# Pooled attention and two-layer network: GpSimd operations begun one per step behind the weights' conversion, bounds' matmuls behind the product with V

## The chip, the cores and the metric

The kernel runs on one core of a Trainium2 chip. The metric is the device time of one execution in microseconds (us), the median of several runs. The program has one launch; its inputs and its output lie in HBM.

## What is computed

Inputs are q, k and v (4 batches, 8 heads, 1152 positions, 64 values per head), a vector `g_ln` (512) and two weight matrices of 512x2048 and 2048x512, all float32. The reference, cut to what matters:

```
q_pool = q.reshape(B, H, S // 2, 2, D).mean(axis=3)
scores = scale * q_pool @ k^T ; attn = softmax(scores)
x   = (attn @ v), heads side by side          # 4 x 576 x 512
xn  = (x - mean) / sqrt(var + 1e-6) * g_ln
out = x + relu(xn @ w_ch1) @ w_ch2
```

## The kernel before, in words

**Tiles and steps.** Two heads of a batch make a pair `p`; there are 16 pairs, four per batch, and each is worked on in 9 steps (`C`) of 128 rows of scores, 144 steps in all. `step(i)` writes out the instructions of step `i` for every engine. There is no scheduler: each engine runs its instructions in the order in which the Python code issues them, and semaphores hold an instruction until what it reads is there. Numbers are split into two float16 halves (high and low), so that TensorE can work in float16 with float32 accuracy.

**The first batch (steps 0 to 35, `on_pe(i)` true).** In a step VectorE takes the maximum of the 1152 scores from PSUM (`emit_max`, L381), ScalarE takes the exponential (L395), TensorE transposes the result (`emit_t`, L428), ScalarE copies it back (L434), and TensorE multiplies it with V in float32 (L452). In the same steps the network's weights are loaded and converted. They come as 32 pieces of 128x1024 (`w_load`), one per step; ScalarE writes an absolute value of one half of the words (`w_bias`, L705) and three VectorE operations per piece (`w_conv`, run by `drip` at L109: a shift, then two combinations of two tiles in SBUF) bring each piece into one part of `wsl`. I call these three the conversion. In `step`, all of them are issued before the low halves of the next pair (L283, L306), which are VectorE's last work in a step.

**The weights' split.** The weights have four parts (0 and 2 of the first matrix, 1 and 3 of the second), each of four slices. When a part's maximum is known, `w_splits(part)` plans three GpSimd operations per slice, on 128x1024 float32: `w_split_a` scales (L257 `wsl<-wsl,gs` or `wsl<-wsl,wscl`), `w_split_b` writes the high half in float16 (L257 `wsl<-wsl`), `w_split_c` subtracts (L788). I call them first product, second product and difference. Parts 0 and 1 are planned in the steps that follow their scale, up to three operations in a step; parts 2 and 3 from steps 36 and 46. `w_done` counts finished slices, and a unit of the network's matmuls is issued only when its slices are counted.

**Other GpSimd work.** For every second pair it adds neighbouring rows of q (`pool_q`, L172) and copies the result (`dup_q`, L178), converts V (`take_v`, L268 to L278), and from step 32 normalises rows (`ln_r`, L551 to L557). From step 36 it computes every third low half of the probabilities (L257 `pe<-pe`, L416), the others run on VectorE (L418).

**Order by tables.** `at(i, fn)` puts a function at the end of step `i`, `pre(i, fn)` at its start.

**Bounds.** To scale a pair, ScalarE sums absolute values of k, q and v (`bound`, L191), TensorE transposes the three sums (`all_max` `one`, L207), VectorE takes their maximum (L210, L211), and TensorE spreads it over the partitions (`two`, L218). `reds` holds these two TensorE pieces for each pair, one per step. From step 36 on, `step` issues TensorE's work in this order: scores of step i+1 (L362, L370), one piece of `reds`, a product with V (`a_piece`, L464, 27 matmuls), a unit of the network (L600 or L632, `some_units`), a transpose for the next pair (`a_prep`).

Of the kernel before, what the change touches and what calls it, by code (L numbers as in the profile page):

```python
# [9 lines left out]
FP32 = mybir.dt.float32  # L10
# [14 lines left out]
def tile_pooled_attention_moe(  # L25
# [18 lines left out]
    nc = tc.nc  # L44
# [4 lines left out]
    C = S // 128  # L49
    HP = H // 2  # L50
# [18 lines left out]
    sm_p = ctx.enter_context(tc.tile_pool(name="sm", bufs=2))  # L69
# [185 lines left out]

    def scaled(dst, src, s=1.0):
        nc.gpsimd.tensor_scalar(dst, src, s, 1.0, op0=ALU.mult, op1=ALU.mult)  # L257

    def take_v(p, h):

# [75 lines left out]
    def on_pe(i):  # L336

        return 0 <= i < HP * C
# [236 lines left out]
    evacs = []  # L575
# [218 lines left out]
    def at(i, fn, *a):  # L794
        todo.setdefault(i, []).append((fn, a))
# [3 lines left out]
    def pre(i, fn, *a):  # L799
        early.setdefault(i, []).append((fn, a))  # L800
# [5 lines left out]
    for p in range(1, NP):  # L806
        i0 = (p - 1) * C
        at(max(i0 - 1, 0), load, p, "k", nc.sync)
        at(i0, load, p, "v", nc.sync)
        at(i0 + 1, bound, p, "k")  # L810
        if p % 2 == 0:
            at(i0 - 2, load_q, p, (nc.sync,))
            pre(i0 + 1, pool_q, p, nc.gpsimd)
            at(i0 + 1, dup_q, p, nc.gpsimd)
            at(i0 + 2, bound, p, "q")
        elif p == 1:
            upper = (64, 64)
            pre(0, behind_scales)
            pre(i0 + 1, pool_q, 1, nc.gpsimd, (upper,))
            at(i0 + 1, dup_q, 1, nc.gpsimd, (upper,))  # L820
            at(i0 + 2, bound, 1, "q", *upper)
        else:
            at(i0 + 1, same_q, p)
        if not on_pe(p * C):
            at(i0 + 2, bound, p, "v")
        pre(i0 + 3, scales_reduce, p, 0, 2 if on_pe(p * C) else 3)
        for n in range(2):
            at(i0 + (5, 7)[n], take_v, p, n)
        for n, (fn, u) in enumerate(PREPS):
            late = 1 if on_pe(i0) else 0  # L830
            pre(i0 + 4 + n + late, lambda fn=fn, p=p, u=u: preps.append((fn, p, u)))
# [8 lines left out]

    this = [0]

    def w_splits(part):
        for n in range(4):
            i0 = this[0] + 1 + 3 * n // 2 if part < 2 else 16 + 10 * part + 5 * n // 2
            for x, fn in ((0, w_split_a), (1, w_split_b), (2, w_split_c)):
                at(i0 + x, fn, 4 * part + n)

# [29 lines left out]
    def norm(i):  # L878

        if not norms or norms[0][1] % 2 == 0 and norms[0][0] != "h" and not room["xn"]:  # L880
            return
        b, t = norms.popleft()
        st = {}
        if b == "h":
            x = xh[t][:, 0]
            dst = xh[t][:, 1].bitcast(FP16).rearrange("p (a n) -> p a n", a=2 * KD)
        else:
            x = xb[b][:, t]
            keep = batch.setdefault(b, {})
            if t % 2 == 0:  # L890
                keep["xn", t] = x_p.tile([128, 2 * KD, 256], FP16, tag="xn", name="xn")
                room["xn"] -= 1
            dst = keep["xn", t - t % 2][:, :, 128 * (t % 2):128 * (t % 2) + 128]
        ln_a(st, x)
        ln_r(st, nc.gpsimd if i < NSTEP else nc.vector)

        def transpose():
            evacs.extend(ln_t(st, dst))

        d = 2 if i < NSTEP else 1  # L900
        at(i + d, transpose)
        if b == "h":
            at(i + d + 1, units_of_half, t)
        elif t % 2:
            at(i + d + 1, units_of, b, t)
            if t == 3 and b == 1:
                at(i + d + 1, lambda: norms.append(("h", 0)))
# [26 lines left out]
    def some_units(i):  # L934
        for _ in range(1 if i < NSTEP + 5 else 2):
            if units and w_done[units[0][0]] >= units[0][1]:
                evacs.extend(units.popleft()[2]())

    def a_piece(i):
        pieces.extend(ready.pop(i, ()))  # L940
        for u in range(2 if len(pieces) > 2 and not on_pe(i) else 1):
            if pieces:
                n = pieces.popleft()
                pt = pts[n]
                ps = emit_pv(n, bank() if u or on_pe(n) else None)
                if on_pe(n):
                    ot = pt.rearrange("p a n -> p (a n)").bitcast(FP32)[0:65, 0:128]
                    evacs.append(lambda ot=ot, ps=ps: nc.scalar.activation(
                        out=ot, in_=ps[0:65, 0:128], func=ACTF.Identity, bias=eps
                    ))  # L950
                    turned.append((n, ot))
                    continue
                evacs.extend(evac_pv(n, ps))
                evacs.append(lambda n=n: evacuated(n))

    def step(i):
        live = i < NSTEP
        this[0] = i
        for fn, a in early.pop(i, ()):
            fn(*a)  # L960
        if live:
            emit_max(i)
        if on_pe(i - 1):
            emit_t_copy(i - 1)
            steps.pop(i - 1)
        while found:
            found.popleft()()
        first = on_pe(i - 2) or on_pe(i)
        if first and not on_pe(i):
            a_piece(i)  # L970
        if on_pe(i):
            if i < 3:
                warm(16, bank())
            a_piece(i)
            a_prep()
            emit_exp(i)
        while scaled_out:
            scaled_out.popleft()()
        if i + 1 < NSTEP:
            emit_s(i + 1)  # L980
            pv_slot[0] = i + 1
        else:
            free_banks[:] = [6, 7, 0, 1, 3, 4]
            pv_slot[0] += 1
        while sums and i % 2 == sums[0][0] // 2:
            sums.popleft()[1]()
        if on_pe(i):
            while fill:
                drip()
            flush()  # L990
        else:
            flush()
            if live:
                emit_exp(i)
                emit_hi(i)
        if 0 <= i - 1 < NSTEP and not on_pe(i - 1):
            emit_lo(i - 1)
            steps.pop(i - 1)
            drip()
        norm(i)  # L1000
        while soon or len(fill) > 3:
            drip()
        if on_pe(i):
            emit_t(i)
            if reds:
                found.append(reds.popleft()())
        elif reds:
            evacs.append(reds.popleft()())
        while turned:
            n, ot = turned.popleft()  # L1010
            emit_turn(n, ot, i)
        if not on_pe(i):
            if not first:
                a_piece(i)
            some_units(i)
            a_prep()
        for fn, a in todo.pop(i, ()):
            fn(*a)

    def warm(n, ps=None):  # L1020
        ps = psum[:, 2, 0:128] if ps is None else ps[:, 0:128]
# [87 lines left out]
```

## Time and profile before

| what | us |
|---|---|
| median of 3 runs (lowest, highest) | 882.64 (880.32, 884.50) |
| profiled execution | 883.46 |
| its span, first to last instruction | 881.7 |
| PE busy | 823.7 |
| VectorE (DVE) busy | 614.7 |
| ScalarE (ACT) busy | 570.7 |
| GpSimd (POOL) busy | 349.0 |

Busy times are sums over the whole span, and the stages have different limits: the first batch with the weights' conversion, batches 1 to 3, and a tail of the network's matmuls. What a change is worth has to be read from its own stage. PE is TensorE's matmuls, PEld its weight loads; a matmul's end is modelled. Time that an engine waits is put down to the instruction that released it.

### The profile page before, as it was taken

The page shows a single profiled execution, that of the slowest core. Times are in us where ns is not written, and L with a number is a line of the kernel's source. Part 1 is how long each engine was busy: PE and PEld are TensorE (multiplying, and loading weights), DVE is VectorE, ACT ScalarE, POOL GpSimd, SP SyncE. Part 2 cuts the span into 40 slices and gives each one's busy share as a digit, 9 for nine tenths or more (in the row PEclk, how much of TensorE's full clock was granted, in tenths as well). Part 3 has the DMA queues.
Part 4 walks back from the last instruction along what each step waited for, and adds up shares of the span by engine and source line. Part 5 has one row for each costly group of instructions (what it writes and reads, how often), then busy time and mean ns, then how long its engine had stood idle before and what let it go on. Part 6 is the DMA issues. An engine that isn't in the chain of part 4 may idle for free.

```text
span 881.7 us, 21840 instructions
## 1 busy us (share of the span) xinstructions
PE 823.7 (93%) x9270; PEld 587.6 (67%) x9270; DVE 614.7 (70%) x1092; ACT 570.7 (65%) x851; POOL 349.0 (40%) x318
## 2 busy tenths in 40 slices
PE   8999899898898999898899999999999999999997
PEld 6778687686656575556666666566757576666764
DVE  4687989897777787778778777777877777532121
ACT  3988788887566686668676767676768676411110
POOL 3010634436776934364464345526343423300000
PEclk9999989899999999999999999999999999999999
DMA  6463436303589698969697969796988967600001
GB/s 187 149 207 120 129 120 183 120 1 87 105 146 181 129 173 162 201 132 181 118 222 124 196 126 215 125 179 113 196 155 158 175 113 135 121 13 13 16 10 24
DMA packets 276017, 115.97 MB, mean 132 GB/s; under 512 B 259280, under 2 KB 259280, under 8 KB 275920
## 3 DMA queue, kind: packets, MB, share of 16 engines
q1 hardware_dynamic: 275568, 113.70, 62.3%
q8 instruction: 72, 1.18, 0.5%
q10 hardware_dynamic: 352, 0.88, 0.4%
q14 instruction: 25, 0.20, 0.1%
HBM read 46.14 MB, written 4.72 MB: 58 GB/s over the span
## 4 chain that ended last, share of the span: by engine, by line
PE 51%; DVE 26%; ACT 13%; DMA 4%; issue 3%; POOL 1%; SPq 1%; ACTq 0%; POOLq 0%; DVEq 0%
PE psum L632 15%; PE psum L600 14%; DVE mx L381 7%; PE psum L464 6%; DVE hl L418 5%; PE psum L362 4%; PE psum L452 4%; ACT pe L395 3%; DVE stage L109 3%; DVE ht L614 2%; PE psum L428 2%; ACT ht L613 2%; DVE wsl L109 2%; PE psum L370 2%; DVE kt L283 1%
## 5 line engine op out<-in xcount | busy, mean ns | idle before, releaser
L381 DVE TENSOR_REDUCE mx<-psum 128x1 f32<-128x1152 f32 x144 | 194.4, 1350 | 20.6 <-ACT xb L519 7.0
L632 PE MATMUL psum<-wsl,ht 128*128 128x512 f16 x864 | 196.6, 379 | 3.9 <-DVE ht L614 3.4
L395 ACT ACTIVATE pe<-psum,nb,sc 128x1152 f32<-128x1152 f32 x144 | 188.9, 1312 | 12.0 <-DVE nb L386 10.5
L600 PEld LDWEIGHTS <-wsl 128*128 128x128 f16 x1920 | 171.9, 99 | 29.5 <-issue 9.2
L600 PE MATMUL psum<-xn,wsl 128*128 128x256 f16 x1536 | 181.7, 277 | 8.4 <-DVE xb L645 4.3
L632 PEld LDWEIGHTS <-ht 128*128 128x128 f16 x864 | 80.8, 98 | 92.3 <-issue 4.5
L409 ACT ACTIVATE hl<-pe 128x1152 f16<-128x1152 f32 x108 | 125.6, 1163 | 8.0 <-DMA pt<-hl 4.7
L362 PE MATMUL psum<-kt,qt 64*128 64x512 f16 (+1 forms) x960 | 127.4, 381 | 1.7 <-ACT pe L395 0.9
L614 DVE SCALAR_TENSOR_TENSOR ht<-psum,ht 128x512 f16<-128x512 f32 x72 | 49.8, 691 | 104.7 <-ACT ht L613 104.7
L464 PE MATMUL psum<-vt,pt 128*128 128x65 f16 (+1 forms) x3240 | 117.6, 194 | 0.0
L464 PEld LDWEIGHTS <-pt 128*128 128x128 f16 (+1 forms) x3240 | 109.5, 100 | 2.5 <-DMA pt<-hl 0.4
L418 DVE SCALAR_TENSOR_TENSOR hl<-pe,hl 128x1152 f16<-128x1152 f32 x72 | 109.3, 1518 | 0.0
L519 ACT ACTIVATE xb<-psum,r 128x64 f32<-128x64 f32 x128 | 39.7, 310 | 96.1 <-DVE r L515 89.0
L613 ACT ACTIVATE ht<-psum 128x512 f16<-128x512 f32 x72 | 42.7, 593 | 88.2 <-PE psum L600 87.9
L257 POOL TENSOR_SCALAR pe<-pe 128x1152 f32<-128x1152 f32 x36 | 42.0, 1168 | 140.1 <-ACT hl L409 135.4
L416 POOL TENSOR_TENSOR hl<-pe,hl 128x1152 f16<-128x1152 f32 x36 | 85.5, 2374 | 3.0
L452 PE MATMUL psum<-pt,vt 128*65 128x128 f32 (+1 forms) x720 | 82.1, 272 | 1.4 <-DVE qt L283 1.4
L452 PEld LDWEIGHTS psum<-pt,vt 128*65 128x65 f32 x720 | 76.1, 144 | 1.8 <-DVE qt L283 1.8
L362 PEld LDWEIGHTS <-qt 64*128 64x128 f16 (+1 forms) x960 | 39.8, 97 | 39.7 <-issue 22.3
L370 PEld LDWEIGHTS <-qt 128*128 128x128 f16 (+1 forms) x320 | 17.8, 99 | 72.5 <-issue 72.0
L370 PE MATMUL psum<-kt,qt 128*128 128x128 f16 (+1 forms) x320 | 41.4, 226 | 12.1 <-ACT xb L519 10.6
L283 DVE SCALAR_TENSOR_TENSOR qt<-psum,s,qt 128x384 f16<-128x384 f32 x48 | 29.5, 614 | 33.3 <-ACT qt L286 33.2
(116 smaller groups left out, 1003.8 us busy)
## 6 DMA issues: line engine op xcount, KB each, us to landing
stage<-in_moe_w_ch_dram SPq DMA_DIRECT2D x32, 512.0 KB, 5.1
kr<-in_k_dram SPq DMA_DIRECT2D x16, 576.0 KB, 4.5
qr<-in_q_dram SPq DMA_DIRECT2D x31, 288.0 KB, 6.2
vr<-in_v_dram SPq DMA_DIRECT2D x15, 576.0 KB, 4.7
out_dram<-xb SPq DMA_DIRECT2D x32, 128.0 KB, 2.5
pt<-hl SPq DMA_TRANSPOSE x108, 4.9
kr<-in_k_dram SPq DMA_DIRECT2D x16, 64.0 KB, 4.2
vr<-in_v_dram ACTq DMA_DIRECT2D x1, 576.0 KB, 6.7
```

What stands on the lines that cost most here:

```text
L362: nc.tensor.matmul(out=sp[o:o + w, c0:c0 + 512], lhsT=qt[r:r + 64, qa, q0:q0 + w], rhs=kt[r:r + 64, ka, h], start=(a == 0), stop=(a == 2),)
L370: nc.tensor.matmul(out=sp[o:o + w, 1024:1152], lhsT=qt[:, qa, q0:q0 + w], rhs=pair[p]["k8"][:, h], start=(qa == 0), stop=(qa == 1),)
L381: nc.vector.tensor_reduce(mx, st["s"], axis=AX.X, op=ALU.max)
L395: nc.scalar.activation(out=st["pe"], in_=st["s"], func=ACTF.Exp, scale=pair[i // C]["sc"][:, 0:1], bias=st["nb"],)
L409: nc.scalar.activation(out=hl[:, 0], in_=st["pe"], func=ACTF.Copy, scale=2.0 ** 15)
L416: nc.gpsimd.tensor_tensor(hl[:, 1], st["pe"], hl[:, 0], op=ALU.subtract)
L418: nc.vector.scalar_tensor_tensor(hl[:, 1], st["pe"], 2.0 ** 15, hl[:, 0], op0=ALU.mult, op1=ALU.subtract)
L452: nc.tensor.matmul(out=ps[0:65, q0:q0 + w], lhsT=vt[:, h, c], rhs=pt[:, 128 * u + q0:128 * u + q0 + w], start=(u == 0), stop=(u == C - 1),)
L464: nc.tensor.matmul(out=dst[:, 0:n], lhsT=lhsT, rhs=rhs, start=(u == 0 and lhsT is hi and n == 65), stop=(u == C - 1 and lhsT is lo), skip_ ...
L600: nc.tensor.matmul(out=ps[:, o:o + n], lhsT=wsl[:, 8 * w + cc, wa, f * 128:f * 128 + 128], rhs=xn[:, xa * KD + cc, 0:n], start=(m == 0), s ...
L614: lambda: nc.vector.scalar_tensor_tensor(lo, pv, 0.0, hi, op0=ALU.max, op1=ALU.subtract),
L632: nc.tensor.matmul(out=ps, lhsT=hv[0][:, ha, f, t * 128:t * 128 + 128], rhs=wsl[:, 8 * w + 4 + f // 2, wa, (f % 2) * DM:(f % 2) * DM + DM] ...
```

## The change

`gate()` is new: VectorE writes one column of a small tile, GpSimd copies it to the next column. Since both engines work in order, what GpSimd has behind the copy can't begin before VectorE has reached its write. A queue `calm` is new as well: at the end of a step one entry is taken from it, with a gate ahead of it (from step 35 on, two entries and no gate). The twelve split operations of parts 0 and 1 go through `calm`, and so do `pool_q` and `dup_q` of pairs 2 and 4; V's conversions of pairs 1 to 3 get a gate of their own. The loads of q for pairs 2 and 4 are issued two steps earlier, the splits of parts 2 and 3 planned from steps 40 and 49. From step 36 on, the piece of `reds` is issued behind the product with V.

```diff
+    def gate():
+        x = sm_p.tile([128, 2], FP32, tag="gate", name="gate", bufs=4)
+        nc.vector.memset(x[:, 0:1], 1.0)
+        nc.gpsimd.tensor_copy(x[:, 1:2], x[:, 0:1])
...
         if p % 2 == 0:
-            at(i0 - 2, load_q, p, (nc.sync,))
-            pre(i0 + 1, pool_q, p, nc.gpsimd)
-            at(i0 + 1, dup_q, p, nc.gpsimd)
+            if on_pe(i0):
+                at(i0 - 4, load_q, p, (nc.sync,))
+                at(i0 - 1, lambda p=p: calm.appendleft((lambda n: pool_q(p, nc.gpsimd), 0)))
+                at(i0, lambda p=p: calm.appendleft((lambda n: dup_q(p, nc.gpsimd), 0)))
+            else:
+                at(i0 - 2, load_q, p, (nc.sync,))
+                pre(i0 + 1, pool_q, p, nc.gpsimd)
+                at(i0 + 1, dup_q, p, nc.gpsimd)
...
         for n in range(2):
+            if on_pe(p * C):
+                at(i0 + (5, 7)[n], gate)
             at(i0 + (5, 7)[n], take_v, p, n)
...
     def w_splits(part):
         for n in range(4):
-            i0 = this[0] + 1 + 3 * n // 2 if part < 2 else 16 + 10 * part + 5 * n // 2
+            if part < 2:
+                calm.extend((fn, 4 * part + n) for fn in (w_split_a, w_split_b, w_split_c))
+                continue
+            i0 = 22 + 9 * part + 5 * n // 2
...
         elif reds:
-            evacs.append(reds.popleft()())
+            red = reds.popleft()
+            put = [None]
+            evacs.append(lambda: put[0]())
...
             if not first:
                 a_piece(i)
+            if red:
+                put[0] = red()
             some_units(i)
             a_prep()
         for fn, a in todo.pop(i, ()):
             fn(*a)
+        if calm and i < HP * C - 1:
+            gate()
+        for _ in range(1 if i < HP * C - 1 else 2):
+            if calm:
+                fn, n = calm.popleft()
+                fn(n)
```

Three places show how the instructions move. First GpSimd's queue around the add for pair 4, in steps 25 to 29; before:

```order
L257 TENSOR_SCALAR wsl<-wsl,wscl 128x1024
L257 TENSOR_SCALAR wsl<-wsl 128x1024
L257 TENSOR_SCALAR wsl<-wsl,wscl 128x1024
L172 TENSOR_TENSOR qr<-qr 128x18x64
L178 COPY qr<-qr 128x18x64
L788 TENSOR_TENSOR wsl<-wsl 128x1024
```

The same place of GpSimd's queue with the change (lines of the changed kernel, where L263 is the gate's copy, L279 V's conversion and L794 the difference):

```order
L263 COPY gate<-gate 128x1
L279 COPY vt<-vr 128x9x64
L263 COPY gate<-gate 128x1
L257 TENSOR_SCALAR wsl<-wsl,gs_84 128x1024
L263 COPY gate<-gate 128x1
L172 TENSOR_TENSOR qr<-qr 128x18x64
L263 COPY gate<-gate 128x1
L178 COPY qr<-qr 128x18x64
L263 COPY gate<-gate 128x1
L257 TENSOR_SCALAR wsl<-wsl 128x1024
```

Each large operation now has a gate's copy in front, and it is still part 0 (`gs`) that is worked on here, where it was part 1 (`wscl`).

Second, VectorE's queue in one step of the first batch with the change (L262 is the gate's write, L387 the maximum, L518 the reciprocal of the row sums; it reads as before but for L262):

```order
L262 MEMSET gate 128x1
L387 TENSOR_REDUCE mx<-psum 128x1
L518 RECIPROCAL r<-psum 128x1
L109 TENSOR_SCALAR stage<-stage 128x512
L109 SCALAR_TENSOR_TENSOR stage<-wsl,stage 128x512
L109 SCALAR_TENSOR_TENSOR wsl<-stage 128x512
L289 SCALAR_TENSOR_TENSOR qt<-psum,s,qt 128x384
```

The write stands behind a step's last work and right ahead of the next step's maximum.

Third, TensorE's queue in a later step in which a pair's bounds are transposed; before:

```order
L370 MATMUL psum<-kt,qt 64x128
L207 MATMUL psum<-ident,acc 3x128
L464 LDWEIGHTS pt
L464 MATMUL psum<-vt,pt 128x65
L464 LDWEIGHTS pt
```

And with the change (L470 is the product with V, L606 the unit):

```order
L470 LDWEIGHTS pt
L470 MATMUL psum<-vt,pt 128x65
L207 MATMUL psum<-ident,acc 3x128
L606 LDWEIGHTS wsl
L606 MATMUL psum<-xn,wsl 128x256
```

The 27 matmuls with V now come ahead of the transpose of the bounds; the number and the order of the units are the same in every step.

## Rows read from the trace of the kernel before

**Rows 1.** Windows by stage: length, busy of PE, PEld, DVE, ACT, POOL; clock, DMA share, GB/s.
```profile
16.05:203.82 187.77, 169.90 (x1667) 141.95 (x1665) 155.72 (x253) 155.59 (x288) 63.90 (x54) 0.95 0.40 129
203.82:300.00 96.18, 84.33 (x936) 57.13 (x933) 72.08 (x128) 64.57 (x90) 70.67 (x57) 0.96 0.70 131
300.00:753.10 453.10, 432.78 (x5463) 292.31 (x5462) 345.36 (x630) 325.56 (x431) 200.09 (x180) 0.99 0.85 160
```
**Rows 2.** Chain that ended last, 16.05 to 203.82 us: shares of that stretch by line.
```profile
by line: PE psum L452 13.6%; DVE stage L109 12.4%; DVE mx L381 10.3%; ACT pe L395 9.5%; PE psum L428 9.4%; DVE wsl L109 7.4%; ACT pt L434 5.0%; PE psum L362 3.3%; issue 2.9%; ACT kt L191 2.4%; DVE kt L283 2.3%; ACT nb L392 2.3%; PE psum L37
```
**Rows 3.** Source L109, the conversion: count, ns min/median/max, first and last start.
```profile
L109 DVE TENSOR_SCALAR stage<-stage x32: 396/409/2315, 35.0 to 199.4; 128x512 int32<-128x512 int32 x32
L109 DVE SCALAR_TENSOR_TENSOR stage<-wsl,stage x32: 676/694/3130, 35.5 to 200.3; 128x512 int32<-128x512 int32 x32
L109 DVE SCALAR_TENSOR_TENSOR wsl<-stage x32: 691/693/2511, 36.2 to 201.0; 128x512 int32<-128x512 int32 x32
```
**Rows 4.** Timeline of DVE and POOL in step 26: start, duration, instruction.
```profile
148.20 2.07 DVE L109 TENSOR_SCALAR stage<-stage 128x512 int32<-128x512 int32 x1
...
147.37 2.62 POOL L172 TENSOR_TENSOR qr<-qr 128x1152 f32<-128x1152 f32 x1
```
**Rows 5.** Windows, one per step with POOL at work: length, DVE time of L109 alone, clock.
```profile
56.05:62.95 6.90, 5.05 (x3) 1.00 0.94 343
...
161.47:166.70 5.23, 3.38 (x3) 0.81 0.53 211
sum 53.30, DVE 35.59; mean DVE 4.45
```
**Rows 6.** Windows over 21 other steps (4 to 8, 10 to 15, 19 to 24, 29 to 32): sums.
```profile
sum 101.74, PE 96.32 PEld 80.35 DVE 81.14 ACT 91.61 POOL 6.14; mean PE 24.08 PEld 20.09 DVE 20.29 ACT 22.90 POOL 1.54
```
**Rows 7.** Timeline of DVE: maximum and first operation of the conversion in steps 19 and 22.
```profile
112.61 1.34 DVE L381 TENSOR_REDUCE mx<-psum 128x1 f32<-128x1152 f32 x1
...
113.94 0.40 DVE L109 TENSOR_SCALAR stage<-stage 128x512 int32<-128x512 int32 x1
...
126.49 1.36 DVE L381 TENSOR_REDUCE mx<-psum 128x1 f32<-128x1152 f32 x1
...
128.97 0.40 DVE L109 TENSOR_SCALAR stage<-stage 128x512 int32<-128x512 int32 x1
```
**Rows 8.** Lines of POOL, 16 to 203.8 us: busy us, mean ns, idle before and its releaser.
```profile
L788 POOL TENSOR_TENSOR wsl<-wsl 128x1024 f16<-128x1024 f32 x8 | 18.7, 2332 | 0.2
L257 POOL TENSOR_SCALAR wsl<-wsl 128x1024 f16<-128x1024 f32 x8 | 10.1, 1257 | 0.7
...
L172 POOL TENSOR_TENSOR qr<-qr 128x1152 f32<-128x1152 f32 x2 | 5.3, 2632 | 33.5 <-DMA qr<-in_q_dram 33.5
L273 POOL COPY vt<-vr 128x576 f32<-128x576 f32 x6 | 4.4, 748 | 5.8 <-DMA vr<-in_v_dram 5.8
...
L194 POOL COPY acc<-acc 128x1 f32<-128x1 f32 x1 | 0.2, 185 | 0.0
```
**Rows 9.** Lines of DVE by shape: the one write of a single column of 128.
```profile
L1034 DVE MEMSET nhalf<- 128x1 f32 x1 | 0.1, 59 | 0.8 <-PEq L1093 0.8
```
**Rows 10.** Waits, 203 to 760 us: us in total, times, longest.
```profile
PE psum L207 <- ACT kt L191: 7.8, 6, 2.1
```
**Rows 11.** Timeline around one of these waits: ACT's last bound, then PE [idle before].
```profile
363.79 0.19 ACT L191 ACTIVATION_READ_ACCUMULATOR kt<-vr 128x1 f32 x1
...
364.03 0.27 PE L207 MATMUL psum<-ident,acc 128*3 128x128 f32 x1 [2.12 <-ACT kt L191]
364.14 1.13 PE L464 MATMUL psum<-vt,pt 128*128 128x65 f16 x27
365.07 1.26 PE L600 MATMUL psum<-xn,wsl 128*128 128x256 f16 x5
```
**Rows 12.** POOL's idle time before 212.38 us, and source L418 (ns min/median/max).
```profile
212.38 0.19 POOL L551 TENSOR_SCALAR rs<-mv 128x1 f32<-128x1 f32 x1 [7.18 <-DVE mv L546]
...
L418 DVE SCALAR_TENSOR_TENSOR hl<-pe,hl x72: 1346/1348/3421, 210.1 to 756.6; 128x1152 f16<-128x1152 f32 x72
```

More of the change, by code (lines that the diff above doesn't have):

```diff
@@ L841, in tile_pooled_attention_moe @@
     this = [0]
+    calm = deque()
     def w_splits(part):
         for n in range(4):
-            i0 = this[0] + 1 + 3 * n // 2 if part < 2 else 16 + 10 * part + 5 * n // 2
+            if part < 2:
+                calm.extend((fn, 4 * part + n) for fn in (w_split_a, w_split_b, w_split_c))
+                continue
+            i0 = 22 + 9 * part + 5 * n // 2
             for x, fn in ((0, w_split_a), (1, w_split_b), (2, w_split_c)):
@@ L1000, in step @@
         norm(i)
+        red = None
         while soon or len(fill) > 3:
```

## The prediction, made before the changed kernel ran

> **What bounds the kernel now.** I read four views, in this order. The windows by stage come first [rows 1]: the reader should see three stages with different limits. In the first batch (187.77 us) no engine is full: PE is busy for 169.90 us, DVE for 155.72, ACT for 155.59. In batches 1 to 3 PE is busy for 432.78 of 453.10 us, so there PE sets the pace, and what makes PE wait costs time. Next I look at the chain of waits in the first batch [rows 2]: the conversion on DVE (L109) holds 12.4% and 7.4% of it, more than any other work but the matmuls with V. It shouldn't: by the view of line L109 its three operations take 409, 694 and 693 ns in the middle case, 1.80 us per step, but 2315, 3130 and 2511 ns in the worst [rows 3]. The timeline of a bad step shows why [rows 4]: GpSimd began an add on q at 147.37 and held it for 2.62 us, and the first operation of the conversion, begun at 148.20, took 2.07 us and ended 0.28 us after the add.
>
> That gives two groups of steps. In steps 9, 16 to 18 and 25 to 28 GpSimd works beside the conversion. These eight take 53.30 us, with 35.59 us of conversion where 8 x 1.80 = 14.4 would do: 21.2 us of DVE time lost [rows 3, 5]. In 21 other steps GpSimd is nearly idle (6.14 us in all), and a step takes 101.74 / 21 = 4.84 us [rows 6]. Eight such steps would be 38.8 us. So **14.5 us** is what the collisions can have cost, and 14.5 / 21.2 = 0.68 is the share of the lost DVE time that the steps felt.
>
> **The change, part by part.**
>
> *Gates ahead of GpSimd's operations.* What is removed: operations that begin anywhere in a step. What is added: 29 writes on DVE of 0.06 us [rows 9], 1.7 us, and 29 copies on GpSimd, of 0.19 us if I take the nearest copy of one column [rows 8]. What moves: an operation now begins just after a step's last DVE work, while DVE takes the next maximum. The maximum reads PSUM, and I see it at 1.34 to 1.36 us with GpSimd busy or not [rows 7, 4]; it is the cover. I estimate the start at 0.3 us behind the maximum's start: the copy, and two handovers of 0.05 us, as between ACT's last bound (ends 363.98) and L207 (364.03) [rows 11]. The conversion begins 1.33 us behind the maximum where nothing makes DVE wait, 2.48 us where DVE waits for ACT [rows 7]. So a product (1.26 us) ends at 1.56, 0.2 us too late in the first kind of step and harmless in the second; a difference (2.33) ends at 2.63, 1.3 or 0.2 too late; an add on q (2.63) at 2.93, 1.6 too late; a product behind a copy of V (0.75 and another gate) at 2.5, 1.2 too late [rows 8].
>
> Counting by the table of steps: two adds (steps 9, 27) 3.2; one difference in a step of the first kind (19) 1.3; three products behind a copy of V (17, 24, 26) 1.2, 0.4 and 1.2; some five other products or copies 0.2 each; three differences in steps of the second kind 0.1 or 0.2 each. That is 8.7 us of DVE time, with the writes 10.4, against 21.2 before. At the share of 0.68 it costs 7.1 us. But a clean step has (101.74 - 81.14) / 21 = 0.98 us of idle DVE [rows 6]; if all of that hides the delay, only what five steps have beyond it is left, some 2 us. I take the middle, 4.5. **Gain 14.5 - 4.5 = 10.0**, between 7.4 and 12.5. In steps 33 to 35 GpSimd also has the normalisation and the V of pair 4, which get no gate, so I expect those steps as they were.
>
> Here the Trainium skill says more. SBUF — State Buffer, section "Who interferes with whom", states that DVE and GpSimd share one pair of SBUF ports as an exclusive lock: whichever starts first keeps it for the whole instruction, and the other is blocked, not slowed. It speaks against the change, because an operation begun first thing in a step then holds DVE until its very end. The trace agrees (2.07 us instead of 0.41, until 0.28 us past the add) [rows 4]. Were the ports shared by halves instead, the residue of 4.5 would be about half, and the sum 2.2 us lower.
>
> *Loads of q two steps earlier.* Eight DMA issues on SP pass two weight loads. Before, the adds waited 33.5 us for q [rows 8], so an add that is to begin at a gate needs this. Weight pieces have four steps, some 19 us, from load to conversion, so they cover it: nothing. If the cover failed, one step would wait some 2 us.
>
> *Hand-over to the second batch.* One operation per step lets the split of part 1 end in step 38 instead of about 34. Its last six operations, without gates from step 35 on, make 2 x 2.33 + 4 x 1.26 = 9.7 us [rows 8] and come where GpSimd was idle for 7.18 us [rows 12]. The units need part 1's last slice in step 44, so PE doesn't wait for it. The low halves on DVE (L418, 1.35 us alone, 3.42 in the worst case) [rows 12] read two tiles in SBUF and are exposed: two such hits cost 4.1, later starts of parts 2 and 3 give some of it back. Between -1 and 4.1 I take 0.5, near the low end since most of the work fits the idle time.
>
> *Bounds behind the product with V.* PE waited 7.8 us for ACT's bounds in six of these transposes [rows 10]. Now the product goes first; it takes from 364.14 to 365.07, 0.93 us [rows 11], so at most 6 x 0.93 = 5.6 us of the wait is covered, less where a wait was shorter. The longest, 2.12, keeps 1.2 in front of the unit: this is what is late next, and every unit of the step is queued behind it. VectorE takes the result only in the next step, behind its maximum, so it loses nothing. In these steps ACT with its bounds is late anyhow and may keep part. Between 0 and 5.6 I take 3.5.
>
> **Sum:** -10.0 + 0 + 0.5 - 3.5 = -13.0. The profiled execution took 883.5 us, 0.8 more than the median of the runs; 883.5 - 13.0 = 870.5, on the median 869.7. I say **870**. With the parts' nearer bounds, my own range is 865 to 876.
>
> **The rivals.**
>
> *The steps were long for another reason (smaller gain).* The eight steps also hold a pair's preparation and a part's scale, and PE's clock was at 0.81 of full in the last [rows 5]; in clean steps PE is busy for 96.32 and ACT for 91.61 of 101.74 us [rows 6], so they may become the limit at once. For it: that thin margin. Against it: L109's share of the chain. At half of 14.5 the gates bring 7.2 - 4.5 = 2.7, with half of the bounds' part 1.8 and the hand-over 0.5: 883.5 - 4.0 = 879.5.
>
> *Everything is hidden (larger gain).* Idle DVE time takes in the residue, and the whole wait of 7.8 goes because the product leaves ACT its time: 883.5 - 14.5 - 7.8 = 861.2. Against it: products shorter than the longest waits.
>
> *The gates don't hold (no gain there).* If GpSimd is behind, an operation starts at the end of the one before and not at its gate, as now; then only the bounds' part is left: 883.5 - 3.5 = 880.0. With at most 2.6 us of work per step of 4.84 it shouldn't fall behind.
>
> *The gate opens late (slower).* Place: GpSimd's copy between DVE's write and the large operation. If it delays the start by more than 1.0 us (1.33 - 0.3), the operation begins with the conversion, and every one of 28 hits it in full: 8 x 2.33 + 18 x 1.26 + 2 x 2.63 = 46.6 us, with the writes 48.3 [rows 8]. Less 0.98 idle in 28 steps, 21 us are felt, at the share of 0.68 33 us, in place of 14.5: 6 to 18 us lost, 3.0 won elsewhere, so 887 to 899, say 893. For it: no gate is in the trace. Against it: the copy of one column at 0.19 us.
>
> The lock in the Trainium skill's page named above would make this case as bad as that: whoever starts first keeps the ports. No run before shows such a start in every step.
>
> **How the numbers follow.** Chances: forecast 0.67, smaller gain 0.14, larger 0.09, gates that don't hold 0.05, slower 0.05. The range of 861 to 881 takes in all but the last, half of the larger gain and some tails. A measurement of this kernel can tell about 0.5%, 4.4 us, from no change. Faster than 878.2 are the forecast, the larger gain and some 0.06 of the smaller: 0.82. The rest of the smaller and the gates that don't hold make 0.13 for the same; slower 0.05.
>
> **What would show it.** Right: the conversion's worst cases at most about 2 us and most at 0.4 and 0.7; steps 16 to 18 and 25 to 28 at 4.7 to 5.7 us; GpSimd's large operations begin about 0.3 us behind a maximum; PE's wait for bounds at L207 down from 7.8 to about 3. Wrong: conversions of 1.4 us in most steps (a late gate), steps still at 6 us with a short conversion (another limit), or the stretch from 204 to 300 us longer by more than 3 us (the hand-over).

## The result, and the profile after

The changed kernel took **870.0 us**, the median of 4 runs (868.86 to 871.78); the kernel before took 883.32 in 4 runs beside it (880.32 to 884.5). The ratio is 0.9856, with a 95% interval of 0.9824 to 0.9888: the change makes the kernel 1.1 to 1.8% faster. The profiled execution took 868.86 us, its span is 867.1, 14.6 less than before.

The windows by stage, with the edges at the same steps as before (length, busy of PE, PEld, DVE, ACT, POOL; clock, DMA share, GB/s), of the changed kernel:

```profile
15.84:190.89 175.05, 162.97 (x1667) 135.36 (x1665) 139.77 (x279) 154.52 (x288) 50.20 (x72) 1.00 0.46 139
190.89:288.20 97.31, 83.03 (x935) 57.33 (x933) 73.67 (x128) 64.93 (x90) 77.88 (x62) 0.98 0.68 129
288.20:738.50 450.30, 430.41 (x5465) 291.19 (x5464) 346.34 (x630) 324.87 (x431) 205.98 (x184) 1.00 0.85 161
```

Against [rows 1] the first batch is 12.72 us shorter, and DVE is busy there for 15.95 us less although it has 26 instructions more. The second stage is 1.13 us longer, the third 2.80 shorter. So nearly all of the gain is in the first batch, and the stage of the hand-over gives a little back.

Source L109, the conversion (count, ns min/median/max), of the changed kernel:

```profile
L109 DVE TENSOR_SCALAR stage<-stage x32: 396/410/2312, 34.8 to 186.5; 128x512 int32<-128x512 int32 x32
L109 DVE SCALAR_TENSOR_TENSOR stage<-wsl,stage x32: 677/694/977, 35.2 to 187.4; 128x512 int32<-128x512 int32 x32
L109 DVE SCALAR_TENSOR_TENSOR wsl<-stage x32: 691/693/1421, 36.0 to 188.1; 128x512 int32<-128x512 int32 x32
```

The middle cases are those of [rows 3]; the worst cases of the second and third operation fell from 3130 and 2511 ns to 977 and 1421. The one shift of 2312 ns that is left stands in step 34, which comes below.

The windows of the eight steps that were long before (9, 16 to 18, 25 to 28), with DVE's time on L109 alone, of the changed kernel:

```profile
55.85:61.01 5.16, 3.30 (x3) 1.00 1.03 382
...
137.00:142.25 5.25, 1.93 (x3) 1.00 0.46 130
142.25:147.72 5.47, 3.30 (x3) 1.00 0.95 294
...
sum 39.63, DVE 17.74; mean DVE 2.22
```

The sum was 53.30 with 35.59 of conversion [rows 5]; it is 13.67 us less, for 17.85 us less of DVE, so that the steps felt 0.77 of what DVE lost. The floor of the conversion is 14.4; of the 3.3 us above it 3.0 stand in steps 9 and 27, which hold the adds on q. The 21 other steps take 101.86 us, against 101.74 [rows 6], though they now hold part of GpSimd's work.

The timeline of DVE and POOL in step 27, where the second add now stands (start, duration, instruction, idle before), of the changed kernel:

```profile
142.25 1.35 DVE L387 TENSOR_REDUCE mx<-psum 128x1 f32<-128x1152 f32 x1
142.28 0.06 DVE L262 MEMSET gate<- 128x1 f32 x1
142.41 0.19 POOL L263 COPY gate<-gate 128x1 f32<-128x1 f32 x1 [3.25 <-DVE gate L262]
142.60 2.62 POOL L172 TENSOR_TENSOR qr<-qr 128x1152 f32<-128x1152 f32 x1
143.60 1.91 DVE L109 TENSOR_SCALAR stage<-stage 128x512 int32<-128x512 int32 x1
```

This is the gate at work. DVE's write and the maximum begin together, the copy ends at 142.60, and the add begins there, 0.35 us behind the maximum. The add ends at 145.22, and the shift, begun at 143.60, ends at 145.51: 0.29 us past the add, 1.5 us longer than alone. The maximum itself, with an add beside it, takes 1.35 us as ever.

Three lines of POOL by shape, 15 to 191 us (busy us, mean ns, idle before), of the changed kernel:

```profile
L794 POOL TENSOR_TENSOR wsl<-wsl 128x1024 f16<-128x1024 f32 x5 | 10.7, 2130 | 0.0
L257 POOL TENSOR_SCALAR wsl<-wsl 128x1024 f16<-128x1024 f32 x5 | 5.2, 1043 | 0.0
L257 POOL TENSOR_SCALAR wsl<-wsl,gs 128x1024 f32<-128x1024 f32 x4 | 4.5, 1118 | 0.0
```

GpSimd's own operations are shorter than in the kernel before: 2.13 us for a difference that took 2.33, 1.04 for a second product of 1.26 [rows 8], 1.12 for a first product of 1.41. That GpSimd, too, can be the one to wait is what experiment 4 shows.

### The profile page after: what moved, and what is told of

The parts are those of the page before. It is cut to its first block, busy times and chain, and to the rows that moved or that the text cites. A ratio compares the mean times of both kernels' runs of the same rounds, so it can differ in the third digit from the quotient of the medians.

```text
span 867.1 us, 21894 instructions
## 1 busy us (share of the span) xinstructions
PE 812.8 (94%) x9270; PEld 579.8 (67%) x9270; DVE 601.3 (69%) x1119; ACT 569.2 (66%) x851; POOL 348.4 (40%) x345
## 4 chain that ended last, share of the span: by engine, by line
PE 44%; DVE 28%; ACT 14%; DMA 6%; issue 4%; POOL 2%; SPq 2%; ACTq 0%; POOLq 0%; DVEq 0%
PE psum L638 14%; PE psum L606 13%; DVE mx L387 8%; DVE hl L424 6%; PE psum L470 4%; PE psum L368 4%; ACT pe L401 4%; PE psum L458 3%; DVE ht L620 3%; ACT ht L619 2%; DMA qr<-in_q_dram 2%; PE psum L434 2%; DVE kt L289 2%; DMA kr<-in_k_dram 2%; ACT xb L525 1%
## 5 line engine op out<-in xcount | busy, mean ns | idle before, releaser
L387 DVE TENSOR_REDUCE mx<-psum 128x1 f32<-128x1152 f32 x144 | 194.7, 1352 | 23.8 <-ACT xb L525 7.8
L606 PEld LDWEIGHTS <-wsl 128*128 128x128 f16 x1920 | 169.7, 98 | 30.0 <-issue 12.1
L606 PE MATMUL psum<-xn,wsl 128*128 128x256 f16 x1536 | 176.4, 273 | 10.6 <-DVE xb L651 5.8
L620 DVE SCALAR_TENSOR_TENSOR ht<-psum,ht 128x512 f16<-128x512 f32 x72 | 49.8, 692 | 99.1 <-ACT ht L619 99.1
L470 PE MATMUL psum<-vt,pt 128*128 128x65 f16 (+1 forms) x3240 | 117.0, 193 | 0.1
L424 DVE SCALAR_TENSOR_TENSOR hl<-pe,hl 128x1152 f16<-128x1152 f32 x72 | 111.1, 1543 | 0.0
L470 PEld LDWEIGHTS <-pt 128*128 128x128 f16 (+1 forms) x3240 | 108.6, 100 | 3.1 <-DMA pt<-hl 0.2
L458 PE MATMUL psum<-pt,vt 128*65 128x128 f32 (+1 forms) x720 | 78.9, 265 | 2.9 <-DVE qt L289 2.9
L458 PEld LDWEIGHTS psum<-pt,vt 128*65 128x65 f32 x720 | 72.9, 140 | 3.4 <-DVE qt L289 3.4
L263 POOL COPY gate<-gate 128x1 f32<-128x1 f32 x27 | 5.2, 192 | 116.8 <-DVE gate L262 116.8
```

The lines of the kernel that those rows point to most:

```text
L387: nc.vector.tensor_reduce(mx, st["s"], axis=AX.X, op=ALU.max)
L424: nc.vector.scalar_tensor_tensor(hl[:, 1], st["pe"], 2.0 ** 15, hl[:, 0], op0=ALU.mult, op1=ALU.subtract)
L458: nc.tensor.matmul(out=ps[0:65, q0:q0 + w], lhsT=vt[:, h, c], rhs=pt[:, 128 * u + q0:128 * u + q0 + w], start=(u == 0), stop=(u == C - 1),)
L470: nc.tensor.matmul(out=dst[:, 0:n], lhsT=lhsT, rhs=rhs, start=(u == 0 and lhsT is hi and n == 65), stop=(u == C - 1 and lhsT is lo), skip_ ...
L606: nc.tensor.matmul(out=ps[:, o:o + n], lhsT=wsl[:, 8 * w + cc, wa, f * 128:f * 128 + 128], rhs=xn[:, xa * KD + cc, 0:n], start=(m == 0), s ...
L620: lambda: nc.vector.scalar_tensor_tensor(lo, pv, 0.0, hi, op0=ALU.max, op1=ALU.subtract),
```

## The experiments

**1. The gates without the bounds' part** (label gates_only) and **2. the bounds' part without the gates** (bounds_only). Together they say which of the two brings the gain, and whether the parts add up.

```diff
-            red = reds.popleft()
-            put = [None]
-            evacs.append(lambda: put[0]())
+            evacs.append(reds.popleft()())
...
-            if red:
-                put[0] = red()
```

> The change without its part on the bounds: the transposes stand ahead of the product with V again. Theory (two parts that add up, the gates the larger): the first batch stays about 13 us shorter, PE's wait at L207 is back at about 7 us, time about 874 (9 to 10 under before). Rival (the bounds' part is swallowed by ACT, which is late in those steps anyhow): 870, as with both parts.

For the second kernel the same lines are put into the kernel before, the other way round.

> The kernel before with the bounds' part alone. Theory: the first batch as before; the wait at L207 falls from 7.8 to about 3 us, time about 879.5 (4 under before). Rival (swallowed by ACT): 883.

Measured: the gates alone 869.76 us (868.19 to 873.35, 4 runs), ratio 0.9877 (0.9841 to 0.9913) to the kernel before on the same chip, 882.08. The bounds' part alone 883.6 (881.53 to 886.43, 10 runs), ratio 1.0026 (1.0005 to 1.0047). So the gates bring the whole gain, and the bounds' part none. Both times are those of the rival, 4 us away from the theory's. But ACT doesn't swallow the part, as the rival had it: it takes time at one place and gives it back at another. The maxima of steps 36 to 38, with their idle time and its releaser; first the changed kernel:

```profile
190.89 1.35 DVE L387 TENSOR_REDUCE mx<-psum 128x1 f32<-128x1152 f32 x1
194.91 1.36 DVE L387 TENSOR_REDUCE mx<-psum 128x1 f32<-128x1152 f32 x1 [2.35 <-PE psum L207]
203.41 1.36 DVE L387 TENSOR_REDUCE mx<-psum 128x1 f32<-128x1152 f32 x1 [2.41 <-PE psum L218]
...
194.42 0.28 PE L486 MATMUL psum<-ident,pt 65*128 65x65 f32 x1 [0.68 <-ACT pe L401]
194.53 0.27 PE L207 MATMUL psum<-ident,wmax 128*1 128x128 f32 x1
```

And the gates alone, steps 36 to 38:

```profile
190.92 1.35 DVE L387 TENSOR_REDUCE mx<-psum 128x1 f32<-128x1152 f32 x1
193.98 1.36 DVE L387 TENSOR_REDUCE mx<-psum 128x1 f32<-128x1152 f32 x1 [1.39 <-PE psum L207]
200.96 1.32 DVE L387 TENSOR_REDUCE mx<-psum 128x1 f32<-128x1152 f32 x1
...
193.60 0.27 PE L207 MATMUL psum<-ident,wmax 128*1 128x128 f32 x1
194.44 0.28 PE L486 MATMUL psum<-ident,pt 65*128 65x65 f32 x1 [0.57 <-ACT pe L401]
```

Both begin step 36 within 0.03 us of each other. In both the next maximum begins 0.11 us behind the end of L207 (194.80 and 194.91; 193.87 and 193.98). The place that L207 writes (`place`) is a stretch of PSUM in the bank that also takes the last of the next step's scores; that the maximum waits on this account is read from the code and not tried. With the bounds' part L207 stands behind the product with V, and here behind L486, which turns a result of the first batch and waits for ACT's exponential. So L207 comes 0.93 us later, and the maximum with it. In the changed kernel step 40 begins at 213.19, 22.30 us behind step 36; with the gates alone it is 209.27, 18.35 behind. Window of steps 36 to 39, of the changed kernel:

```profile
190.89:213.19 22.30, 17.05 (x143) 12.84 (x141) 15.60 (x27) 15.35 (x23) 18.10 (x17) 0.92 0.39 89
```

Not all of the 3.95 us is the order of the instructions. The granted clock is 0.92 here (0.50, or 1.2 GHz, from 197.0 to 200.4), and with the gates alone it is 1.00, with PE busy for 15.29 us and not 17.05. In the second profile of the gates alone (experiment 8) the clock was 0.91 in these four steps, and they took 20.02 us. So at a like clock the bounds' part costs some 2.3 us here.

Most of it is paid back later. Step 66 begins at 348.83 with the change and 346.34 with the gates alone, step 72 at 383.88 and 383.20: 1.4 us have come back by step 66, and 1.8 more in the steps where PE's longest wait of 2.12 us stood [rows 11]. Windows of steps 66 to 71, of the changed kernel and then of the gates alone:

```profile
348.83:383.88 35.05, 31.43 (x390) 21.47 (x387) 25.62 (x53) 24.92 (x35) 17.30 (x20) 1.00 0.81 161
346.34:383.20 36.86, 32.77 (x390) 22.35 (x387) 25.70 (x53) 25.33 (x35) 17.35 (x20) 0.95 0.80 154
```

Here, too, most of the difference is the clock: 1.34 of the 1.81 us are busy time of PE, with the same 390 matmuls. With the gates alone PE waits for 2.15 us ahead of L207 at 351.14, and the granted clock is 0.50 from 351.5 to 354.9; with the change the wait is 0.85 us and the clock stays at 1.00.

Elsewhere PE's wait has only changed its name. Waits of PE over batches 1 to 3, of the kernel before (300 to 753 us) and of the changed kernel (288 to 738), as us, times, longest; before:

```profile
PE psum L207 <- ACT kt L191: 6.8, 5, 2.1
...
PE psum L600 <- DVE xb L645: 2.3, 2, 1.5
...
PE psum L563 <- DVE ht L614: 2.0, 2, 1.1
```

The changed kernel (L606 is L600, L569 is L563, L620 is L614, L651 is L645):

```profile
PE psum L606 <- DVE xb L651: 4.2, 3, 1.9
PE psum L569 <- DVE ht L620: 3.8, 3, 1.7
...
PE psum L207 <- ACT kt L191: 1.8, 4, 0.8
```

The wait for ACT at L207 fell by 5.0 us, while the units and the transposes of normalised rows wait 3.7 us longer for DVE. All of PE's waits on other engines in this stretch sum to 20.0 us before and 19.7 after. That the stretch is 2.80 us shorter all the same is PE's busy time, 2.37 us less at a clock of 1.00 where it was 0.99.

**3. The change without the gates** (no_gate). The one operation per step, the earlier loads and the bounds' part stay; only the order between DVE and GpSimd goes.

```diff
-        if calm and i < HP * C - 1:
-            gate()
...
-            if on_pe(p * C):
-                at(i0 + (5, 7)[n], gate)
```

> The change without its gates: one operation per step is still issued, but nothing holds GpSimd to the step. Theory (the gate does it): GpSimd runs ahead as before, the collisions in the first batch come back, its conversion again takes some 20 us too much, time 880 to 883. Rival (issuing one operation per step, the earlier loads and the later parts 2 and 3 do it): about 870.

Measured: 882.42 us (880.29 to 886.24, 10 runs), ratio 1.0018 (0.9993 to 1.0042). Source L109, one of its three operations, without the gates:

```profile
L109 DVE SCALAR_TENSOR_TENSOR stage<-wsl,stage x32: 675/694/3025, 35.8 to 199.6; 128x512 int32<-128x512 int32 x32
```

The timeline of POOL where part 0's split begins, without the gates:

```profile
97.26 1.27 POOL L257 TENSOR_SCALAR wsl<-wsl,gs 128x1024 f32<-128x1024 f32 x1 [22.90 <-DVE r L518]
98.61 1.36 POOL L257 TENSOR_SCALAR wsl<-wsl 128x1024 f16<-128x1024 f32 x1
100.06 2.44 POOL L794 TENSOR_TENSOR wsl<-wsl 128x1024 f16<-128x1024 f32 x1
```

Spreading the operations over the steps in the code does nothing by itself: GpSimd was idle for 22.90 us until DVE released it, and then ran the operations of several steps back to back. The worst conversions are back, and so is the time. Without the gates nothing of the gain is left; what gates would bring without the spreading was not tried.

This run also says what PE's clock had to do with it. Before, the granted clock was low in three of the collided steps (18, 27 and 28) and in two others (11 and 19). Windows over all engines of the kernel before, steps 18 and 27:

```profile
106.28:112.61 6.33, 4.29 (x35) 3.77 (x36) 6.26 (x8) 3.97 (x8) 6.16 (x5) 0.70 0.33 101
154.95:161.47 6.52, 4.49 (x39) 4.01 (x40) 6.42 (x10) 4.18 (x8) 6.35 (x5) 0.63 0.31 113
```

In both PE was busy for under 4.5 of 6.3 to 6.5 us, and DVE for all but 0.1 us, so there was little that a faster PE could have shortened. With the change the first batch has a clock of 1.00 where it had 0.95 [rows 1], and PE is busy for 6.93 us less with the same 1667 matmuls. Without the gates the first batch ran at 0.99:

```profile
16.41:203.15 186.74, 165.51 (x1667) 137.32 (x1665) 150.80 (x253) 155.14 (x288) 50.34 (x46) 0.99 0.41 130
```

It still took 186.74 us, 1.03 less than before and 11.69 more than with the gates. So the higher clock is not what gave the 12.72 us. What it is worth exactly stays open, because the conversion, too, was 5.05 us shorter in this run than before (77.46 against 82.51 in all).

**4. The gate late** (late_gate). The same operations, one per step, with the same gate, but both issued right ahead of the conversion and not ahead of the maximum. This makes the slow rival's case.

```diff
         if on_pe(i):
+            if calm and i < HP * C - 1:
+                gate()
+                fn, n = calm.popleft()
+                fn(n)
             while fill:
                 drip()
...
-        if calm and i < HP * C - 1:
-            gate()
-        for _ in range(1 if i < HP * C - 1 else 2):
+        for _ in range(0 if i < HP * C - 1 else 2):
```

> The change with the gate opened late: in the first batch the gate and its operation are issued right ahead of the step's conversion instead of behind it, so that each of some 20 operations of the weights' split and q begins with a conversion. Theory (a collision costs the operation's length less the idle 0.98 us that DVE has in a step): products 0.2 us each, differences 1.2, adds on q 1.6, in all 10 to 18 us over the change, 880 to 888. Rival (0.68 of the length is felt, as in the eight steps of before): 20 to 30 us over the change, 890 to 900. Second rival (the place in the step doesn't matter, only that one operation runs per step): 870.

Measured: 879.46 us (876.49 to 881.1, 10 runs), ratio 0.9976 (0.9959 to 0.9994). Timeline of DVE and POOL in two steps with the late gate:

```profile
103.16 0.42 DVE L109 TENSOR_SCALAR stage<-stage 128x512 int32<-128x512 int32 x1
103.18 0.06 DVE L262 MEMSET gate<- 128x1 f32 x1
103.58 2.14 POOL L794 TENSOR_TENSOR wsl<-wsl 128x1024 f16<-128x1024 f32 x1
103.61 2.67 DVE L109 SCALAR_TENSOR_TENSOR stage<-wsl,stage 128x512 int32<-128x512 int32 x1
...
109.25 1.62 POOL L257 TENSOR_SCALAR wsl<-wsl,gs 128x1024 f32<-128x1024 f32 x1
109.25 0.70 DVE L109 SCALAR_TENSOR_TENSOR stage<-wsl,stage 128x512 int32<-128x512 int32 x1
109.99 1.41 DVE L109 SCALAR_TENSOR_TENSOR wsl<-stage 128x512 int32<-128x512 int32 x1
```

In the first step GpSimd was 0.03 us ahead: the difference took its usual 2.14 us, and DVE's operation took 2.67 instead of 0.69, until 0.56 us past it. In the second both are recorded at 109.25, and the product took 1.62 us instead of 1.12, while DVE's operation kept its 0.70; the next one on DVE then waited. So it went with all four first products of part 0, and the differences and second products went as in the first step. The conversion took 85.16 us in all, 19.6 more than the 65.57 with the change, and the first batch 184.60 us, 9.55 more: 0.49 of DVE's loss was felt. So the position in the step is worth 9.5 us. The time lies just below the 880 to 888 of my theory and far from both rivals.

**5. The bounds' part only from step 41 on** (bounds_late). If its loss lies in steps 36 to 40 and its gain later, leaving out the early steps should beat both the change and the gates alone.

```diff
-            red = reds.popleft()
-            put = [None]
-            evacs.append(lambda: put[0]())
+            if i < HP * C + 5:
+                evacs.append(reds.popleft()())
+            else:
+                red = reds.popleft()
+                put = [None]
+                evacs.append(lambda: put[0]())
```

> The change, but in steps 36 to 40, where rows of the first batch are still turned back, the transposes of the bounds stand ahead of the other work again; from step 41 on they stand behind the product with V. Theory (the bounds' part gives 1.5 to 2 us back near step 68 and loses 2 to 3 us in steps 36 to 38, where the maximum waits for L207 and L218 and these for ACT's exponential): the maximum's waits in steps 37, 38 and 40 fall from 5.7 to about 1.4 us, and the time is 867 to 868.5. Rival (the order of these few steps only moves a wait, and the bounds' part is worth nothing anywhere): 870, as the change and as the gates alone.

Measured: 868.06 us (866.19 to 870.11, 5 runs), ratio 0.9847 (0.9822 to 0.9871). Windows of steps 33 to 35 and 36 to 39, of this kernel:

```profile
173.20:190.75 17.55, 14.63 (x163) 12.16 (x161) 16.40 (x27) 12.77 (x26) 14.70 (x19) 1.00 0.09 26
190.75:209.10 18.35, 15.29 (x140) 11.21 (x137) 14.57 (x28) 14.12 (x22) 15.60 (x16) 1.00 0.46 106
```

Steps 36 to 39 take 18.35 us at a clock of 1.00, as before the change and with the gates alone; with the change they took 22.30 at 0.92. Step 72 begins at 381.19, 2.0 us ahead of the gates alone: the late gain is kept.

**6. The loads of q as before** (loads_late), two steps before the pair and not four.

```diff
-                at(i0 - 4, load_q, p, (nc.sync,))
+                at(i0 - 2, load_q, p, (nc.sync,))
```

> The change with the loads of q for pairs 2 and 4 issued where they were, two steps later. Theory (an add that stands behind a gate needs its q by then): the add of step 9 starts when q lands, some 1.4 us later, inside the conversion, and costs 1 to 2 us; the one of step 27 likewise or not at all; 871 to 873. Rival (no matter): 870.

Measured: 871.19 us (867.86 to 871.95, 4 runs), ratio 0.9869 (0.9836 to 0.9902); the interval doesn't separate it from the change. The trace does, in one step. Timeline of the add in step 9:

```profile
57.98 2.64 POOL L172 TENSOR_TENSOR qr<-qr 128x1152 f32<-128x1152 f32 x1 [1.34 <-DMA qr<-in_q_dram]
58.08 3.09 DVE L109 SCALAR_TENSOR_TENSOR stage<-wsl,stage 128x512 int32<-128x512 int32 x1
```

The gate was open, but q wasn't there: the add began 1.34 us late, beside the conversion, and the step took 6.06 us, against 5.16. The first batch took 176.04 us, 0.99 more than with the change. The second add was not late. So the earlier load is needed, for about 1 us.

**7. No split operation in steps 32 to 34** (skip_v, on top of experiment 5). There the normalisation and the V of pair 4 also run on GpSimd, without a gate. The timeline of step 34 of the changed kernel:

```profile
177.95 1.25 POOL L284 TENSOR_TENSOR vt<-vr,vt 128x576 f16<-128x576 f32 x1
...
179.28 2.13 POOL L794 TENSOR_TENSOR wsl<-wsl 128x1024 f16<-128x1024 f32 x1
179.39 2.31 DVE L109 TENSOR_SCALAR stage<-stage 128x512 int32<-128x512 int32 x1
```

The maximum of this step begins at 177.92. The ungated conversion of V behind it pushed the gated difference to 179.28, 1.36 us behind the maximum and 0.11 us ahead of the shift, which took 2.31 us. Steps 33 to 35 took 17.59 us with the change and 16.76 before, 0.8 us more and not the 1.5 of the expectation below.

```diff
-        if calm and i < HP * C - 1:
+        many = 0 if i in (32, 33, 34) else 1 if i < HP * C - 1 else 2
+        if calm and many == 1:
             gate()
-        for _ in range(1 if i < HP * C - 1 else 2):
+        for _ in range(many):
```

> As bounds_late, and in steps 32 to 34 no split operation is taken from the queue, because GpSimd has the normalisation and V of pair 4 there; the three go into steps 35 to 39, two per step, without gates. Theory (in steps 33 to 35 the ungated operations collide with the conversion, the change lost 1.5 us there against the kernel before): these three steps shorten by 1.5 to 2 us, the hand-over has no conversion left to collide with, 865.5 to 867. Rival (the collisions move to the low halves of the second batch, L424, and the units wait): 868 to 871.

Measured: 868.14 us (867.35 to 869.48, 4 runs), ratio 0.9848 (0.9823 to 0.9874), the same as experiment 5 and above the 865.5 to 867 that I expected. The two windows of experiment 5, of this kernel:

```profile
173.69:189.80 16.11, 14.43 (x163) 12.20 (x162) 13.85 (x23) 12.88 (x26) 11.09 (x16) 1.00 0.13 39
189.80:209.70 19.90, 16.85 (x140) 12.77 (x137) 14.74 (x27) 14.11 (x22) 17.00 (x15) 0.91 0.40 89
```

The collision is gone, 1.44 us of it, but steps 36 to 39 take 1.55 us more. That is not the work of the three operations: PE is busy for 1.56 us longer with the same 140 matmuls, at a granted clock of 0.91 where it was 1.00, and idle for as long as in experiment 5. The gates alone, which leave these operations where they were, had the same 0.91 and 20.02 us in one of their two profiles. Whether moving the operations brings the low clock is not shown, and the runs show no gain from it.

**8. Three kernels on one chip**: the change (all_same_chip), the gates alone (gates_same_chip), the bounds' part from step 41 on (bounds_late_same_chip), since the medians above come from different chips.

> The change itself, beside the next two on one chip. Theory (the bounds' part gives as much as it takes): ratio to before 0.985 to 0.986, the same as the gates alone within 1 us. Rival (the bounds' part is worth something): 2 us or more under the gates alone.

> The gates alone, on the same chip. Theory: within 1 us of the change, and about 2 us over the kernel in which the bounds' part acts from step 41 on. Rival (the part is worth nothing anywhere): all three alike.

> The change with the bounds' part from step 41 on, on the same chip. Theory: 2 us under both others, since it keeps the gain near step 68 and not the loss in steps 36 to 38. Rival: no difference that five rounds can tell.

| kernel | median us (lowest to highest, runs) | ratio to before (95%) | span of the profiled run |
|---|---|---|---|
| before | 881.43 (879.36 to 884.23, 11) | | |
| the change | 870.41 (867.92 to 871.41, 4) | 0.9864 (0.9838 to 0.9889) | 869.6 |
| the gates alone | 870.02 (868.17 to 877.46, 6) | 0.9879 (0.9848 to 0.9910) | 868.9 |
| bounds' part from step 41 on | 867.24 (866.32 to 870.76, 4) | 0.9845 (0.9820 to 0.9869) | 864.5 |

The change and the gates alone can't be told apart. The third is some 3 us lower in its median, and the spans of its two profiled runs, here and in experiment 5 (864.5, 864.4), are below those of the change (869.6, 867.1) and of the gates alone (868.9, 866.4). Its interval overlaps theirs, so it is probably the better version, but the runs don't prove it; it beats the kernel before by 1.3 to 1.8%.

## Why the prediction was right, and where it was not

The forecast was 870 us, and 870.0 was measured. The mechanism it named carries the gain, but two of its terms missed in opposite directions, so that the number is better than the working.

**The gates: right in kind, too small.** The step was "Gain 14.5 - 4.5 = 10.0", and the first batch gained 12.7. The 12.7 are 13.67 us won in the eight steps, less 0.83 in steps 33 to 35 and 0.12 in the 21 others. So the 14.5 of collisions nearly stands. What failed is the residue, "That is 8.7 us of DVE time". The adds came out as worked out (1.5 us each, 1.6 forecast) and step 19 nearly (1.0, 1.3 forecast). But for three products behind a copy of V I had 1.2, 0.4 and 1.2; steps 17 and 26 show 0.23 and 0.13, and the "five other products" show nothing. The lengths were means of [rows 8], and these means already held the collisions that the change removes: a product takes 1.04 or 1.12 us and not 1.26, a copy of V 0.67 and not 0.75. And I let the conversion begin 1.33 us behind the maximum, where in step 26 it began 1.90 behind. The bound of 12.5, "if all of that hides the delay", was the better value, but more because the delays weren't there than because they were hidden. The count was off as well: the two parts have 24 split operations, and of these and the four on q only 21 get a gate, with six gates ahead of V's conversions 27 in all and not 29.

**The lock.** The Trainium skill (SBUF — State Buffer, section "Who interferes with whom") states that DVE and GpSimd share a pair of ports exclusively and that the order of issue decides who is blocked. The runs agree on the first: the shift behind the add ended 0.29 us past it. On the second they agree where one was clearly ahead (by 0.03 us in the late gate's first step); where both are recorded at the same time, GpSimd's product lost, and why it did is not shown. In the same section the Trainium skill states that a reduction like the maximum never contends. The trace agrees: the maximum stayed at 1.32 to 1.36 us in every step. The sum with ports shared by halves would have had 12.2 for the gates, nearer to the measured 12.7 than my 10.0; it falls all the same, because the two adds cost 1.5 us each, as with the lock, and the rest of what was won came from products that cost nothing.

**Loads of q: right.** Nothing was lost to them, and without them the add in step 9 is late and the step loses about 1 us.

**Hand-over: 0.5 forecast, 0 measured at its place.** With the gates alone steps 36 to 39 take the 18.35 us that they took before, as long as the clock is 1.00; in their second profile it was 0.91, and they took 20.02. I had expected steps 33 to 35 "as they were"; they lost 0.8 us, because ungated work pushed a gated operation into the conversion.

**Bounds: wrong.** "VectorE takes the result only in the next step, behind its maximum, so it loses nothing" is the sentence that failed, and -3.5 the term. At step 37 the maximum itself waits for the transpose (0.11 us behind it in both orders). Steps 36 to 39 took 3.95 us longer, some 1.7 of it by a lower clock; 3.2 came back by step 72, part of that by a higher clock, which was in no term of mine; and most of the wait that went at L207 in batches 1 to 3 turned into PE's waits for DVE. Together the part is worth nothing: 1.0026 of the time alone, and no difference on top of the gates. I noted ACT's wait as what is late next in the one long case, but not that DVE is late right behind ACT in the others.

**The sum by the trace.** Step 36 begins 12.9 us earlier than before, step 60 10.5, step 72 12.3, and the end 14.6. Of the last 2.3 us 1.9 lie in steps 100 to 116, which took 93.07 us before and 91.13 after. In the profile of the kernel before PE waited there for 1.73 us, until 548.79, and the granted clock was 0.50 from 549.1 to 552.5. The gates alone, with the same order of PE's work as before, had neither and took 90.77. So most of this belongs to the profiled run of the kernel before and not to the change.

**The rivals.** Of the smaller gain's reason, that PE or ACT become the limit at once, the eight steps show nothing: those without an add take 4.5 to 5.3 us. The larger gain (861) was nearly right on the conversion and wrong on the bounds. "The gates don't hold" has its twin in experiment 3, at 882 us. The slow rival's mechanism is real, but its price was not. It had 28 hits where 21 operations stand behind such a gate, and "at the share of 0.68 33 us"; experiment 4 shows 19.6 us of DVE and 9.5 felt, a share of 0.49. In part of the hits GpSimd was the one to wait (the four first products of part 0 took 1.62 us each in the mean). That kernel took 879 us and not 893, 0.2% under the kernel before.

## What to carry to other kernels

Where two engines lock each other out, the place at which an operation begins can matter more than how much of it there is: a tiny write and a tiny copy, 0.25 us together, put GpSimd's work under a VectorE operation that reads PSUM and isn't locked, and that was worth 12 us, while spreading the work in the code without it was worth nothing. Take lengths from undisturbed instances and not from means, when the disturbance is what the change removes. And before an instruction is moved back in an engine's queue, look in the trace for who else waits for it, not only who uses its result. When two profiles of a stretch differ, compare the granted clock first: a short stretch at half of it made most of two differences here that looked like the work's order.

## What the hardware showed that was not expected

- GpSimd's operations are lengthened as well: a product took 1.62 us instead of 1.12 where DVE's two-input operation began at the same time, and the gate's copy of one column 0.30 instead of 0.19 beside a shift. I had counted only what DVE loses.
- PE's granted clock was lower in some collided steps before (0.70 and 0.63, with PE busy for two thirds of the step), and 1.00 in the first batch after. It gave back 6.93 us of PE's busy time, but a run at 0.99 without the gates still took 186.74 us there.
- A long wait of PE could cost more than itself. In the profiles of the kernel before and of the gates alone (two), PE waited for 2.07 to 2.15 us ahead of L207 in step 66, and behind it the granted clock fell to 0.50 (1.2 GHz); steps 66 to 71 took 36.8 to 36.9 us, at 0.95 in the mean. In the nine profiles with the bounds' part there the wait was 0.8 to 1.5 us and the clock stayed at 1.00; these steps took 35.0 to 35.7 us.
